# Routing counts of a capacity MoE with the operands swapped: eight-column float32r choices stationary, and the low parts of g moved to VectorE

## The chip, the core and the metric

One core of a Trainium2 chip runs the whole program. The metric is device time in microseconds (us) of one execution, from the first to the last instruction and a little around it. The engines are TensorE (PE, with its weight loads as PEld), VectorE (DVE), ScalarE (ACT), GpSimd (POOL) and SyncE (SP, which issues most DMAs).

## What is computed

Three layers follow one another on 1792 tokens: an attention with normalised queries and keys, a hardswish MLP (768 to 2048 to 768 features), and a mixture of 8 experts in which each expert takes at most 224 tokens.

```python
logits = x @ w_gate                       # 1792 x 8
order = np.argsort(-logits.flatten())
for idx in order:                         # best (token, expert) pairs first
    tok, e = idx // E, idx % E
    if assigned[tok] >= 0 or counts[e] >= cap:
        continue
    assigned[tok] = e
    counts[e] += 1
for e in range(E):
    mask = assigned == e
    out[mask] = np.maximum(x[mask] @ w1[e], 0.0) @ w2[e]
```

## The kernel before

Float32 products are made of float32r parts: a matrix is split into a high part (ScalarE copies it into float32r) and a low part (the difference), and three products high-high, high-low and low-high are added up.

The work runs in stages. Attention and the first MLP product are interleaved first. Then comes the second MLP product, called the y stage here: 14 tiles of 128 tokens, each with 16 blocks of 128 features, three products for each, in two column halves of 512 and 256 (`y_mm`, L1118). That is 14 x 16 x 3 x 2 = 1344 matmuls. Twelve tiles are done with both halves in turn; of the last two tiles first the 512-column halves are done, then the 256-column ones. Last come the experts.

The operand g of the y stage is read back from DRAM by `load_g` in units of four feature blocks (128 x 512 numbers). ScalarE makes the high part g2h (L1059), and GpSimd the low part g2l (L1061). There are two buffers for g2h and g2l, so g2h of a unit waits until TensorE has finished with the unit two before it. One unit feeds 24 y matmuls.

The routing (`routing`, L816 to L1026) is a Python generator that runs inside the y stage: each `yield` says how many y matmuls come before the next piece of routing on TensorE (the tuple `Y`, L62). TensorE's order is the order of the program text. The other engines' orders from the y stage on are planned at build time from estimated durations: an instruction that is ready may be put ahead of one that is not. On the chip each engine keeps its planned order.

The routing computes the greedy assignment by rounds: there are E - 1 = 7 of them and each fills one expert. A round finds each token's best open expert (`best`, giving the one-hot matrix A of 128 partitions x 14 token columns x 8 experts), turns the chosen logits into sortable keys of two 16-bit halves (kh, kl), and finds for all experts at once the largest key threshold at which some expert is full. Each half is found in three digits of 40 possible values. One digit is one step, so a round has 6 steps and the kernel 42:

- VectorE compares every key with 40 thresholds: C, 128 x 14 x 40 (L923).
- TensorE counts: 14 matmuls with C stationary (40 columns) and A moving (8 columns), giving 40 x 8 counts (L928).
- VectorE compares the counts with the room left: G, 40 x 8 (L930).
- TensorE adds G up over its 40 partitions and spreads the sum to 128 partitions, a matmul with `ones` (L933).
- VectorE takes the largest of 8 sums (js, L935), adds it to the prefix (L936), and shifts the thresholds (L921).

Before a step's counts stand Y[1] = 11 y matmuls, before its L933 Y[2] = 3. After six steps come counts above and at the threshold (L938 to L950), the choice of the expert and the ties (L953 to L972), and the update of what is open (L974 to L984), behind Y[3] = 16, Y[4] = 17 and Y[5] = 27 y matmuls. All counted numbers are small whole numbers, held in bfloat16. After the rounds the slots of the tokens are worked out (L986 to L1026). Per round 6 x 14 + 16 + 17 + 27 = 144 y matmuls are given, in all 30 + 7 x 144 + 10 + 20 = 1068. The routing starts when the router's logits are complete, 176 y matmuls into the stage, and has to end before the gather of the first expert's tokens, which needs the y of all tokens.

Of the kernel before, what the change touches and what calls it, by code (L numbers as in the profile page):

```python
# [8 lines left out]
F32 = mybir.dt.float32  # L9
# [12 lines left out]
def kernel(  # L22
# [39 lines left out]
    Y = (30, 11, 3, 16, 17, 27, 10, 20)  # L62
# [753 lines left out]
    def routing():  # L816
# [3 lines left out]
        DIG = ((40, (41 * 41, 41, 1)),) * 2  # L820
# [9 lines left out]
        tri = t_([128, 128], "tri", BF16)  # L830
        V.tensor_scalar(tri, jp[:, :128], 0.0, None, op0=OP.is_gt)
        ones = t_([128, 128], "ones", BF16)
        V.memset(ones, 1.0)
# [37 lines left out]
        V.tensor_copy(Lw, L)  # L871
        U = t_([128, NTC], "U")
# [12 lines left out]
        def best():  # L885
            m = t_([128, NTC], "m")
            V.tensor_reduce(m, Lw, axis=AX.X, op=OP.max)
            w = t_([128, NTC, E], "w")
            V.tensor_tensor(w, Lw, bc(m), op=OP.is_equal)
            V.tensor_tensor(w, w, be(e8), op=OP.mult)  # L890
            V.tensor_reduce(m, w, axis=AX.X, op=OP.max)
            A = t_([128, NTC, E], "A", BF16)
            V.tensor_tensor(A, w, bc(m), op=OP.is_equal)
            return A

        yield Y[0]
        for r in range(E - 1):
            A = best()
            w = t_([128, NTC, E], "w")
            kh = t_([128, NTC], "kh")  # L900
            kl = t_([128, NTC], "kl")
            V.tensor_tensor(w, A, hi, op=OP.mult)
            V.tensor_reduce(kh, w, axis=AX.X, op=OP.add)
            V.tensor_tensor(w, A, lo, op=OP.mult)
            V.tensor_reduce(kl, w, axis=AX.X, op=OP.add)
            V.tensor_tensor(kh, kh, U, op=OP.mult)
            found = []
            for key, (J, steps) in zip((kh, kl), DIG):
                if key is kl:
# [5 lines left out]
                p = t_([128, 1], "pre" + ("h" if key is kh else "l"))  # L915
                V.memset(p, 0.0)
                for i, x in enumerate(steps):
                    thr = jt[x][:, :J]
# [17 lines left out]
                    V.scalar_tensor_tensor(p, js, float(x), p, op0=OP.mult, op1=OP.add)  # L936
                found.append(p)
            gt = t_([128, NTC], "gt")  # L938
            ge = t_([128, NTC], "ge")
            V.tensor_scalar(gt, kl, found[1], None, op0=OP.is_gt)  # L940
            V.tensor_scalar(ge, kl, found[1], None, op0=OP.is_ge)
            rg = t_([128, 2, E], "rg")
# [3 lines left out]
            rgb = t_([128, 2, E], "rgb", BF16)  # L946
            V.tensor_copy(rgb, rg)
            yield Y[3]
            n = psum(128, 2 * E)
            nc.tensor.matmul(n, ones, rgb.rearrange("p a e -> p (a e)"), start=True, stop=True)  # L950
            es = t_([128, E], "es")
            m1 = t_([128, 1], "m1")
            V.tensor_tensor(es, n[:, E:], cap, op=OP.is_ge)  # L953
            V.tensor_tensor(es, es, e8, op=OP.mult)
            V.tensor_reduce(m1, es, axis=AX.X, op=OP.max)
            V.tensor_scalar(es, es, m1, None, op0=OP.is_equal)
            V.tensor_tensor(cap, cap, n[:, :E], op=OP.subtract)
# [4 lines left out]
            V.tensor_tensor(w, A, be(es), op=OP.mult)  # L962
            T = t_([128, NTC], "T")
            V.tensor_reduce(T, w, axis=AX.X, op=OP.add)
            V.tensor_tensor(ge, ge, gt, op=OP.subtract)
            V.tensor_tensor(T, T, ge, op=OP.mult)
            Tb = t_([128, NTC], "Tb", BF16)
            V.tensor_copy(Tb, T)
# [3 lines left out]
            nc.tensor.matmul(n, tri, Tb, start=True, stop=True)  # L972
            cc = t_([128, NTC, NTC], "cc")
# [4 lines left out]
            V.tensor_tensor(T, T, cum, op=OP.mult)  # L978
            V.tensor_tensor(gt, gt, T, op=OP.add)
            V.tensor_tensor(U, U, gt, op=OP.subtract)  # L980
            V.tensor_tensor(w, A, bc(gt), op=OP.mult)
            V.tensor_tensor(asg, asg, w, op=OP.add)
            V.scalar_tensor_tensor(cap, es, 9999.0, cap, op0=OP.mult, op1=OP.add)
            V.scalar_tensor_tensor(Lw, be(es), -3.0e38, Lw, op0=OP.mult, op1=OP.add)  # L984
            yield Y[5]
        A = best()  # L986
# [13 lines left out]
        tot = t_([128, E], "tot", BF16)  # L1000
# [25 lines left out]
        V.scalar_tensor_tensor(sidx, n[:, :2 * E], 128.0, lo, op0=OP.mult, op1=OP.add)  # L1026

# [88 lines left out]
    def y_mm(f, n, a, w, hf):  # L1116
# [8 lines left out]
        elif cnt[0] >= cnt[1]:  # L1125
            cnt[1] = cnt[0] + next(route, 10 ** 9)

# [186 lines left out]
```

## Time and profile before

| | |
|---|---|
| median of 3 runs | 1180.79 us (1177.22 to 1183.72) |
| the profiled execution, whole | 1180.09 us |
| its span, first to last instruction | 1178.2 us |
| mean granted TensorE clock | 0.985 of full speed |
| y stage, all of it | from 602.5 to 899 us |
| of it with routing, first count to slot numbers | from 646.8 to 883.3 us |

Times in the rows are microseconds from the first instruction. A group row gives busy time, mean duration of one instruction in ns, and the engine's idle time just before with what ended it. In a timeline a row with "x2" merges two instructions of the same kind. Matmuls are pipelined: the distance between starts is what one costs, not its duration.

### The profile page before, as it was taken

The page shows a single profiled execution, that of the slowest core. Times are in us where ns is not written, and L with a number is a line of the kernel's source. Part 1 is how long each engine was busy: PE and PEld are TensorE (multiplying, and loading weights), DVE is VectorE, ACT ScalarE, POOL GpSimd, SP SyncE. Part 2 cuts the span into 40 slices and gives each one's busy share as a digit, 9 for nine tenths or more (in the row PEclk, how much of TensorE's full clock was granted, in tenths as well). Part 3 has the DMA queues.
Part 4 walks back from the last instruction along what each step waited for, and adds up shares of the span by engine and source line. Part 5 has one row for each costly group of instructions (what it writes and reads, how often), then busy time and mean ns, then how long its engine had stood idle before and what let it go on. Part 6 is the DMA issues. An engine that isn't in the chain of part 4 may idle for free.

```text
span 1178.2 us, 19479 instructions
## 1 busy us (share of the span) xinstructions
PE 1114.9 (95%) x7204; PEld 903.5 (77%) x7204; DVE 707.3 (60%) x1485; ACT 519.4 (44%) x941; POOL 488.6 (41%) x363
## 2 busy tenths in 40 slices
PE   3988999999999999999999999999997999999997
PEld 2777765766766667787777777777777899999997
DVE  7887877886677844212432666666674756555560
ACT  3655655744545555543441111111123666565551
POOL 2211455663445533113452222222234577766540
PEclk9998999989999999999999999999999999999999
DMA  4365899978787887669995222222235888777731
GB/s 122 106 187 149 223 289 273 315 233 288 244 256 249 262 281 249 211 196 339 311 325 159 60 67 73 68 68 73 60 102 153 250 264 262 229 228 221 232 124 43
DMA packets 212678, 230.95 MB, mean 196 GB/s; under 512 B 26276, under 2 KB 185704, under 8 KB 212584
## 3 DMA queue, kind: packets, MB, share of 16 engines
q1 hardware_dynamic: 209256, 218.71, 60.3%
q0 software_dynamic: 3328, 11.01, 3.1%
q8 instruction: 56, 0.92, 0.3%
q14 instruction: 38, 0.31, 0.1%
HBM read 178.63 MB, written 51.04 MB: 195 GB/s over the span
## 4 chain that ended last, share of the span: by engine, by line
PE 71%; DVE 12%; DMA 7%; issue 5%; ACT 3%; POOL 2%; SPq 1%; POOLq 0%; DVEq 0%; ACTq 0%
PE y L1118 17%; PE h L528 17%; PE y L1266 8%; PE h L1202 5%; PE st L335 4%; PE av L424 3%; PE h L1204 3%; PE av L375 2%; PE rt L928 2%; DMA we_s<-in_moe_w_dram 2%; DMA w_hl<-w 2%; PE s L313 1%; DVE C L923 1%; PE lg L570 1%; DMA w<-cv 1%
## 5 line engine op out<-in xcount | busy, mean ns | idle before, releaser
L528 PE MATMUL h<-xh,w 128*128 128x448 f32 x768 | 241.7, 385 | 0.9 <-DVE mx L316 0.5
L528 PEld LDWEIGHTS h<-xh,w 128*128 128x128 f32 x768 | 144.3, 192 | 36.2 <-issue 21.9
L1061 POOL TENSOR_TENSOR g2l<-gr,g2h 128x512 fp32r<-128x512 f32 x60 | 78.8, 1315 | 190.2 <-ACT g2h L1059 154.9
L528 PE MATMUL h<-xl,w 128*128 128x448 f32 x384 | 146.8, 382 | 0.0
L1059 ACT ACTIVATE g2h<-gr 128x512 fp32r<-128x512 f32 x60 | 37.8, 631 | 221.6 <-PE y L1118 168.3
L316 DVE TENSOR_REDUCE mx<-s 112x1 f32<-112x448 f32 x192 | 105.7, 611 | 44.7 <-PE s L313 44.7
L1118 PE MATMUL y<-woh,g2l 128*128 128x512 f32 (+1 forms) x448 | 127.6, 347 | 1.0 <-POOL g2l L1061 1.0
L1118 PE MATMUL y<-woh,g2h 128*128 128x512 f32 (+1 forms) x448 | 126.8, 347 | 0.0
L1118 PE MATMUL y<-wol,g2h 128*128 128x512 f32 (+1 forms) x448 | 125.7, 345 | 0.0
L118 POOL TENSOR_TENSOR wel<-we_s,weh 128x768 fp32r<-128x768 f32 x48 | 97.8, 2041 | 42.7 <-ACT weh L117 31.9
L118 DVE TENSOR_TENSOR wel<-we_s,weh 128x768 fp32r<-128x768 f32 x59 | 79.3, 1350 | 58.3 <-ACT weh L117 58.1
L117 ACT ACTIVATE weh<-we_s 128x768 fp32r<-128x768 f32 x107 | 88.3, 840 | 56.7 <-DMA we_s<-in_moe_w_dram 40.4
L346 ACT ACTIVATE ph<-st 112x448 f32<-112x448 f32 x192 | 92.9, 544 | 44.6 <-PE st L335 43.8
L417 POOL TENSOR_TENSOR pa<-ph 112x448 f32<-112x448 f32 x68 | 85.7, 1282 | 41.6 <-ACT ph L346 41.6
L1202 PE MATMUL h<-xe,weh 128*128 128x448 f32 x318 | 100.4, 375 | 2.7 <-DVE xe L1153 2.7
L528 PEld LDWEIGHTS h<-xl,w 128*128 128x128 f32 x384 | 73.8, 192 | 12.4 <-issue 7.2
L1118 PEld LDWEIGHTS y<-woh,g2h 128*128 128x128 f32 x448 | 71.8, 188 | 11.8 <-issue 2.5
L1118 PEld LDWEIGHTS y<-woh,g2l 128*128 128x128 f32 x448 | 72.1, 188 | 11.1 <-POOL g2l L1061 1.3
L1118 PEld LDWEIGHTS y<-wol,g2h 128*128 128x128 f32 x448 | 71.7, 188 | 9.8 <-issue 0.7
L1204 PE MATMUL h<-xe,wel 128*128 128x224 f32 x318 | 76.6, 268 | 0.0
L531 ACT ACTIVATE r<-h,half 128x448 f32<-128x448 f32 x64 | 40.6, 635 | 80.5 <-PE h L528 70.2
L1266 PE MATMUL y<-weh,hl 128*112 128x384 f32 x216 | 72.9, 338 | 0.0
(244 smaller groups left out, 2311.4 us busy)
## 6 DMA issues: line engine op xcount, KB each, us to landing
we_s<-in_moe_w_dram SPq DMA_DIRECT2D x128, 384.0 KB, 3.9
w<-w_hl SPq DMA_DIRECT2D x32, 768.0 KB, 5.0
gr<-g_dr SPq DMA_DIRECT2D x52, 256.0 KB, 2.9
wraw<-in_moe_w_in_dram SPq DMA_DIRECT2D x16, 768.0 KB, 6.7
win_v<-w SPq DMA_DIRECT2D x32, 384.0 KB, 7.9
w_hl<-w SPq DMA_DIRECT2D x16, 768.0 KB, 5.5
wraw<-in_moe_w_out_dram SPq DMA_DIRECT2D x16, 768.0 KB, 5.5
g_dr<-g SPq DMA_DIRECT2D x48, 224.0 KB, 4.4
```

Source lines behind the costliest of these rows:

```text
L117: nc.scalar.activation(hi, raw, AF.Copy)
L118: eng.tensor_tensor(lo, raw, hi.bitcast(F32), op=OP.subtract)
L316: mx = nc.vector.tensor_reduce(MX[i][:, s, c:c + 1], pp[s][:CP, :S], axis=AX.X, op=OP.max)
L335: nc.tensor.matmul(pp[s][:CP, :S], a[r], b[r], start=(n == 0), stop=(n == len(todo) - 1))
L346: nc.scalar.activation(e, pp[s][:CP, :S], AF.Exp)
L417: nc.gpsimd.tensor_tensor(PA[i, s, n], PP[i, s, 2 * n][0], PP[i, s, 2 * n + 1][0], op=OP.add)
L528: nc.tensor.matmul(p[:, :S], lhs[:, c], x[:, c], start=(n == 0), stop=(n == 3 * NC - 1))
L1061: eng.tensor_tensor(gl, g, gh.bitcast(F32), op=OP.subtract)
L1118: nc.tensor.matmul(pp[hf][:, :COLS[hf].stop - COLS[hf].start], a[:, f % QF], w[:, COLS[hf]], start=(f == 0 and n == 0), stop=(f == NF - 1 ...
L1202: mm = [lambda: nc.tensor.matmul(p[:, :4 * CP], wh[:, fo], x.rearrange("d k t -> d (k t)"), start=(c == 0), stop=(c == NC - 1), skip_group ...
L1204: lambda: nc.tensor.matmul(p[:, :2 * CP], wl[:, fo], x[:, 0], start=False, stop=False, skip_group_check=True)]
L1266: nc.tensor.matmul(p[:CP, :HW], a[:, f, tk], w[:, o], start=(f == 0 and n == 0), stop=(f == FB - 1 and n == 2))
```

## The change

The roles in the counting matmul are exchanged: A is now stationary (128 x 8) and C moving (128 x 40), all in float32r. Before the 14 matmuls stands one that subtracts the room left (`capn` with `c128`), so that the counts are compared with zero. The comparison GZ is a 128 x 40 tile of which 8 partitions are written and the rest stay zero, and the matmul with `ones` uses all 128 partitions. VectorE then compares the sums with zero (g), adds up 40 numbers instead of taking the largest of 8, and subtracts the prefix inside the comparison that makes C, without shifting thresholds. In each round the update of the logits and the next `best` are issued behind the tie matmuls, before the ties are cut, and the two reductions of counts above and at the threshold become one over a tile of 2 x 14 x 8. While the routing runs the low parts of g are VectorE instructions, issued one at a time behind C, or forced when more than two wait; outside the routing GpSimd makes them as before. The y matmuls given become Y = (30, 12, 3, 12, 6, 31, 44, 22), with 4 more before the first count of the low half; in all 30 + 7 x (6 x 15 + 4 + 12 + 6) + 6 x 31 + 44 + 22 = 1066.

```diff
-    Y = (30, 11, 3, 16, 17, 27, 10, 20)
+    Y = (30, 12, 3, 12, 6, 31, 44, 22)
...
-                        thr = t_([128, JM], "thr")[:, :J]
-                        V.tensor_scalar(thr, jt[x][:, :J], p, None, op0=OP.add)
-                    C = t_([128, NTC, JM], "C", BF16)[:, :, :J]
-                    V.tensor_tensor(C, key[:, :, None].to_broadcast([128, NTC, J]),
-                                    thr[:, None, :].to_broadcast([128, NTC, J]), op=OP.is_ge)
-                    yield Y[1]
-                    n = psum(J, E)
+                        V.scalar_tensor_tensor(C, kb, p, jb, op0=OP.subtract, op1=OP.is_ge)
+                    else:
+                        V.tensor_tensor(C, kb, jb, op=OP.is_ge)
+                    if d == 0 and i == 0:
+                        kl = keys(A, lo, "kl")
+                    elif d == 0 and i == 1 and r:
+                        assign(*old)
+                    else:
+                        low_part()
+                    yield Y[1] + (4 if d and not i else 0)
+                    n = psum(E, JM)
+                    nc.tensor.matmul(n, capn[:, 1], c128[:, :JM], start=True, stop=False)
                     for c in range(NTC):
-                        nc.tensor.matmul(n, C[:, c, :], A[:, c, :], start=(c == 0), stop=(c == NTC - 1))
-                    G = t_([JM, E], "G", BF16)[:J]
-                    V.tensor_tensor(G, n, cap[:J], op=OP.is_ge)
+                        nc.tensor.matmul(n, AR[:, c, :], C[:, c, :], start=False, stop=(c == NTC - 1))
+                    V.tensor_scalar(GZ[:E], n, 0.0, None, op0=OP.is_ge)
                     yield Y[2]
-                    n = psum(128, E)
-                    nc.tensor.matmul(n, ones[:J, :], G, start=True, stop=True)
+                    n = psum(128, JM)
+                    nc.tensor.matmul(n, ones, GZ, start=True, stop=True)
+                    g = t_([128, JM], "g")
+                    V.tensor_scalar(g, n, 0.0, None, op0=OP.is_gt)
                     js = t_([128, 1], "js")
-                    V.tensor_reduce(js, n, axis=AX.X, op=OP.max)
+                    V.tensor_reduce(js, g, axis=AX.X, op=OP.add)
...
-            for i, x in enumerate((gt, ge)):
-                V.tensor_tensor(w, A, bc(x), op=OP.mult)
-                V.tensor_reduce(rg[:, i], w.rearrange("p c e -> p e c"), axis=AX.X, op=OP.add)
+            V.tensor_tensor(w2, A[:, None].to_broadcast([128, 2, NTC, E]),
+                            gg[:, :, :, None].to_broadcast([128, 2, NTC, E]), op=OP.mult)
...
+                V.tensor_reduce(rgb, w2.rearrange("p a c e -> p a e c"), axis=AX.X, op=OP.add)
...
+            nc.tensor.matmul(rn, c128, capn.rearrange("p a e -> p (a e)"), start=True, stop=False)
+            nc.tensor.matmul(rn, ones, rgb.rearrange("p a e -> p (a e)"), start=False, stop=True)
...
+            V.scalar_tensor_tensor(Tb, m, m1, ge, op0=OP.is_equal, op1=OP.mult)
...
             nc.tensor.matmul(n2, ones, Tb, start=True, stop=True)
             nc.tensor.matmul(n, tri, Tb, start=True, stop=True)
+            V.scalar_tensor_tensor(Lw, be(es), -3.0e38, Lw, op0=OP.mult, op1=OP.add)
+            old = A, gt
+            m, AR, A = best()
...
+    def low_part(eng=None, keep=1):
+        while len(lows) > keep:
+            gl, g, gh = lows.pop(0)
+            (eng or nc.vector).tensor_tensor(gl, g, gh.bitcast(F32), op=OP.subtract)
+            if eng is None:
+                break
...
-        eng = nc.gpsimd
-        eng.tensor_tensor(gl, g, gh.bitcast(F32), op=OP.subtract)
         GU[t, i] = gh, gl
+        lows.append((gl, g, gh))
+        if not routed[0]:
+            low_part(nc.gpsimd, 0)
+        elif len(lows) > 2:
+            low_part(nc.vector, 2)
```

## Rows read from the trace of the kernel before

**Rows 1.** The page, part 4: shares of the span in the chain that ended last.
```profile
PE y L1118 17%; PE h L528 17%; PE y L1266 8%; PE h L1202 5%; PE st L335 4%; PE av L424 3%; PE h L1204 3%; PE av L375 2%; PE rt L928 2%; DMA we_s<-in_moe_w_dram 2%; DMA w_hl<-w 2%; PE s L313 1%; DVE C L923 1%; PE lg L570 1%; DMA w<-cv 1%
```

**Rows 2.** By stretch: length, busy time of PE, PEld, DVE, ACT, POOL; clock, DMA share.
```profile
646.00:884.00 238.00, 231.81 (x1705) 184.39 (x1704) 155.07 (x533) 35.20 (x58) 62.11 (x48) 1.00 0.26 71
```

**Rows 3.** PE timeline of one step, 649.9 to 653.6: start, us, then the instruction.
```profile
649.86 0.40 PE L1118 MATMUL y<-wol,g2h 128*128 128x512 f32 x1
650.18 0.51 PE L928 MATMUL rt<-A,C 128*40 128x8 bf16 x14
650.62 0.39 PE L1118 MATMUL y<-wol,g2h 128*128 128x256 f32 x1
650.85 0.51 PE L1118 MATMUL y<-woh,g2l 128*128 128x512 f32 x2
651.29 0.18 PE L933 MATMUL rt<-G,ones 40*128 40x8 bf16 x1
651.39 0.62 PE L1118 MATMUL y<-woh,g2h 128*128 128x512 f32 x2
...
653.59 0.51 PE L928 MATMUL rt<-A,C 128*40 128x8 bf16 x14
```

**Rows 4.** The chain in order of time: y matmuls that nothing interrupts.
```profile
607.88 10.88 PE y L1118 x63
```

**Rows 5.** PEld timeline: weight loads of the counts, of y, of `ones`.
```profile
650.18 0.42 PEld L928 LDWEIGHTS <-C 128*40 128x40 bf16 x14 [0.25 <-issue]
650.62 0.19 PEld L1118 LDWEIGHTS y<-wol,g2h 128*128 128x128 f32 x1
668.45 0.10 PEld L950 LDWEIGHTS <-ones 128*128 128x128 bf16 x1 [0.17 <-issue]
```

**Rows 6.** Timeline: three full 128 x 128 transposes between y matmuls.
```profile
607.15 0.40 PE L1118 MATMUL y<-wol,g2h 128*128 128x512 f32 x1
607.17 0.47 PEld L596 LDWEIGHTS t<-ident,lgs 128*128 128x128 f32 x3
607.63 0.36 PE L1118 MATMUL y<-wol,g2h 128*128 128x256 f32 x1
607.84 0.40 PE L1118 MATMUL y<-woh,g2l 128*128 128x512 f32 x1
```

**Rows 7.** PE timeline, expert stage, float32r of 224 columns; chain: float32 of 66.
```profile
1026.04 0.26 PE L1204 MATMUL h<-xe,w 128*128 128x224 f32 x1
1026.14 0.37 PE L1202 MATMUL h<-xe,w 128*128 128x448 f32 x1
54.35 1.53 PE av L375 x16
```

**Rows 8.** PE's waits for other engines from 646 to 884: total, times, longest.
```profile
PE rt L928 <- DVE C L923: 3.0, 7, 0.4
PE rt L971 <- DVE Tb L968: 1.6, 1, 1.6
PE rt L1004 <- DVE tot L1001: 0.9, 1, 0.9
```

**Rows 9.** Timeline of DVE and POOL: C in a step undisturbed, and beside g2l.
```profile
648.78 0.74 DVE L923 TENSOR_TENSOR C<-kh,thr 128x560 bf16<-128x560 f32 x1
650.73 0.16 DVE L930 TENSOR_TENSOR G<-rt,cap 40x8 bf16<-40x8 f32 x1 [1.21 <-PE rt L928]
658.96 1.29 POOL L1061 TENSOR_TENSOR g2l<-gr,g2h 128x512 fp32r<-128x512 f32 x1 [4.51 <-ACT g2h L1059]
658.99 1.86 DVE L923 TENSOR_TENSOR C<-kl,thr 128x560 bf16<-128x560 f32 x1
```

**Rows 10.** A line's DVE instructions, the whole run: duration min/median/max in ns.
```profile
L118 DVE TENSOR_TENSOR wel<-we_s,weh x59: 942/959/3910, 890.8 to 1137.8; 128x768 fp32r<-128x768 f32 x59
```

**Rows 11.** DVE timeline from the tie matmuls to the next round's C.
```profile
672.12 0.36 DVE L974 TENSOR_TENSOR cc<-ctri,rt 128x196 f32<-128x196 f32 x1 [0.26 <-PE rt L972]
677.45 0.73 DVE L923 TENSOR_TENSOR C<-kh,jt 128x560 bf16<-128x560 f32 x1
```

More of the change, by code (lines that the diff above doesn't have):

```diff
@@ L828, in psum @@
             return ps.tile([128, 512], F32, name="rt", tag="b", bufs=8)[:p, :n]
-        tri = t_([128, 128], "tri", BF16)
+        tri = t_([128, 128], "tri", F32R)
         V.tensor_scalar(tri, jp[:, :128], 0.0, None, op0=OP.is_gt)
-        ones = t_([128, 128], "ones", BF16)
-        V.memset(ones, 1.0)
+        ones = t_([128, 128], "ones", F32R)
+        V.memset(ones.bitcast(F32), 1.0)
+        GZ = t_([128, JM], "GZ", F32R)
+        V.memset(GZ.bitcast(F32), 0.0)
+        c128 = t_([128, 128], "c128", F32R)
+        V.memset(c128.bitcast(F32), 1.0 / 128)
         ji = t_([128, JM], "ji", I32)
@@ L891, in best, with keys, assign @@
             V.tensor_reduce(m, w, axis=AX.X, op=OP.max)
-            A = t_([128, NTC, E], "A", BF16)
+            A = t_([128, NTC, E], "A", F32R, 2)
             V.tensor_tensor(A, w, bc(m), op=OP.is_equal)
-            return A
+            return m, A, A.bitcast(F32)
+        def keys(A, part, name):
+            w = t_([128, NTC, E], "w")
+            key = t_([128, NTC], name)
+            V.tensor_tensor(w, A, part, op=OP.mult)
+            V.tensor_reduce(key, w, axis=AX.X, op=OP.add)
+            return key
+        def assign(A, x):
+            w = t_([128, NTC, E], "w")
+            V.tensor_tensor(w, A, bc(x), op=OP.mult)
+            V.tensor_tensor(asg, asg, w, op=OP.add)
+        V.tensor_scalar(capn[:, 1], cap, -1.0, None, op0=OP.mult)
+        m, AR, A = best()
+        kh = keys(A, hi, "kh")
         yield Y[0]
         for r in range(E - 1):
[L898 to L905, printed above, removed]
             V.tensor_tensor(kh, kh, U, op=OP.mult)
             found = []
-            for key, (J, steps) in zip((kh, kl), DIG):
-                if key is kl:
+            for d, steps in enumerate(DIG):
+                if d:
                     hs = found[0]
@@ L914, in routing @@
                     V.tensor_tensor(kl, kl, t, op=OP.add)
-                p = t_([128, 1], "pre" + ("h" if key is kh else "l"))
-                V.memset(p, 0.0)
+                key = kl if d else kh
+                p = t_([128, 1], f"pre{d}")
                 for i, x in enumerate(steps):
-                    thr = jt[x][:, :J]
+                    C = t_([128, NTC, JM], "C", F32R)
+                    kb = key[:, :, None].to_broadcast([128, NTC, JM])
+                    jb = jt[x][:, None, :].to_broadcast([128, NTC, JM])
@@ L934, in routing @@
+                    g = t_([128, JM], "g")
+                    V.tensor_scalar(g, n, 0.0, None, op0=OP.is_gt)
                     js = t_([128, 1], "js")
-                    V.tensor_reduce(js, n, axis=AX.X, op=OP.max)
-                    V.scalar_tensor_tensor(p, js, float(x), p, op0=OP.mult, op1=OP.add)
+                    V.tensor_reduce(js, g, axis=AX.X, op=OP.add)
+                    if i:
+                        V.scalar_tensor_tensor(p, js, float(x), p, op0=OP.mult, op1=OP.add)
+                    else:
+                        V.tensor_scalar(p, js, float(x), None, op0=OP.mult)
@@ L946, in routing @@
-            rgb = t_([128, 2, E], "rgb", BF16)
-            V.tensor_copy(rgb, rg)
+            w2 = t_([128, 2, NTC, E], "wg2")
+            V.tensor_tensor(w2, A[:, None].to_broadcast([128, 2, NTC, E]),
+                            gg[:, :, :, None].to_broadcast([128, 2, NTC, E]), op=OP.mult)
+            rgb = t_([128, 2, E], "rgb", F32R)
+            with nc.allow_low_precision(reason="counts up to 14"):
+                V.tensor_reduce(rgb, w2.rearrange("p a c e -> p a e c"), axis=AX.X, op=OP.add)
@@ L948, in routing @@
+            V.tensor_tensor(ge, ge, gt, op=OP.subtract)
             yield Y[3]
-            n = psum(128, 2 * E)
-            nc.tensor.matmul(n, ones, rgb.rearrange("p a e -> p (a e)"), start=True, stop=True)
+            rn = psum(128, 2 * E)
+            nc.tensor.matmul(rn, c128, capn.rearrange("p a e -> p (a e)"), start=True, stop=False)
+            nc.tensor.matmul(rn, ones, rgb.rearrange("p a e -> p (a e)"), start=False, stop=True)
             es = t_([128, E], "es")
             m1 = t_([128, 1], "m1")
-            V.tensor_tensor(es, n[:, E:], cap, op=OP.is_ge)
@@ L977, in routing @@
             V.scalar_tensor_tensor(cum, n, rem, cum, op0=OP.subtract, op1=OP.is_lt)
-            V.tensor_tensor(T, T, cum, op=OP.mult)
+            T = t_([128, NTC], "T")
+            V.tensor_tensor(T, Tb.bitcast(F32), cum, op=OP.mult)
             V.tensor_tensor(gt, gt, T, op=OP.add)
             V.tensor_tensor(U, U, gt, op=OP.subtract)
[L981 to L986, printed above, removed]
+            if r < E - 2:
+                yield Y[5]
+        assign(*old)
         w = t_([128, NTC, E], "w")
@@ L999, in routing @@
             s = s2
-        tot = t_([128, E], "tot", BF16)
+        tot = t_([128, E], "tot", F32R)
         V.tensor_copy(tot, s[:, NTC - 1])
@@ L1125, in y_mm @@
         elif cnt[0] >= cnt[1]:
+            routed[0] = 1
             cnt[1] = cnt[0] + next(route, 10 ** 9)
+            if cnt[1] > 10 ** 8:
+                routed[0] = 0
+                low_part(nc.gpsimd, 0)
     XR, XE, got, EP = {}, {}, [None], []
```

27 lines of the change are left out of this document (14 added, 13 removed).

## Prediction

> **What bounds the kernel now.** I read the page's chain first: what ended last runs for 17% of the span through the y matmuls and for 2% through the counting matmuls [rows 1]. So a change inside the y stage counts in full where it shortens TensorE's own sequence, and hardly anywhere else. Then I read the stretch with the routing: 238 us, TensorE busy 231.8, VectorE 155.1, GpSimd 62.1, the clock at 1.00 of full speed [rows 2]. The reader should see that VectorE has some 80 us to spare and TensorE has 6. What TensorE waits for there, by the list of waits, is short: 3.0 us for C, 1.6 for Tb, 0.9 for tot [rows 8]. The waits are not the main cost. That is seen only in the timeline of one step: from one group of counts to the next, 650.18 to 653.59, pass 3.41 us for 14 y matmuls [rows 3]. Uninterrupted ones take 10.88 / 63 = 0.173 us each [rows 4], so 14 take 2.42. The other 0.99 us, 42 times, some 42 us in all, is what two small groups of matmuls cost TensorE.
>
> **Where the 0.99 us lie.** A pair of y matmuls (512 and 256 columns) takes 0.346 by [rows 4]; by its columns two thirds of it, 0.23, are the first's and 0.115 the second's. In [rows 3] the counts start 0.32 after a 512-column matmul, 0.09 late; 14 of them run until the next y at 650.62, 0.44; the next 256-column one takes 0.23, 0.11 too long. Sum 0.64. Around L933 the pair in front takes 0.44 (0.09 late) and the matmul with ones 0.10; the rest of the 0.99, 0.16, lies behind it, where the next y loads its weights anew as it does behind the counts. I round to 0.66 for the counts and 0.33 for the ones. The delay in front goes with the weight load: the loads of L928 and L950 begin only after 0.25 and 0.17 us of an idle loader [rows 5], so they did not run under the y matmul before them. The loads of the three full-width transposes did: the first begins at 607.17, while the y matmul of 607.15 streams, and the three cost 607.84 - 607.15 - 0.346 = 0.34, or 0.115 each, with hardly any delay in front [rows 6].
>
> **Part 1, the ones matmul.** It becomes 128 x 128 and float32r. I take it to behave like a transpose of [rows 6]: 0.115, and 0.13 with a small margin, instead of 0.33. That is 42 x 0.20 = 8.4 us less. Its bounds: 42 x 0.215 = 9.0 less, or, if the load still starts late and lasts as long as the y matmul's own load of that width and type (0.19 against 0.10 [rows 5], so 0.1 more), 42 x 0.1 = 4.2 more. The Trainium skill (TensorE: Matmul & The Clock Gate, section Weight-path perf modes) speaks against this part: the fast weight load needs 128 weights and a type that is not FP32, so the float32r ones would lose it. By that rule alone the sum would have the 4.2 more. No row here shows whether the load that is lost is also the one that can't overlap.
>
> **Part 2, the counts.** Fifteen pairs of load and matmul instead of 14. In the old group 14 loads take 0.42; less 0.10, about one load's own length, they follow each other by 0.32 / 13 = 0.025 us [rows 5]. An 8-column load is shorter than a 40-column one, and 40 float32r columns at the pace of 224 in 0.10 us [rows 7] are 0.018, both under 0.025. So I take 0.025: one pair more, 42 x 0.025 = 1.1 us. I leave the delays before and behind (0.09, 0.11), since the tile is as narrow as before. The bounds: float32, not float32r, of 66 columns on a 112-column load costs 1.53 / 16 = 0.096 a pair [rows 7], so 15 x 0.096 - 0.35 = 1.09 a step, 46 us more, at the far end; and if a narrow float32r load does overlap, 42 x 0.30 = 12.6 us less. I take the low value because the float32r row has over three times the 66 columns in the same time. The Trainium skill (FP8 and Floating Point Precision, TensorE Precision Notes) gives true FP32 four passes; with four passes 40 columns would be 0.067 by that page, an estimate. The float32r row of 224 columns shows one pass, and no row is narrower.
>
> **Part 3, rn and the ties.** Two more full-width matmuls take the place of one per round, and two others change type: by 0.115 each [rows 6] nothing or 0.1 less per round. I count 0.4 less.
>
> **Part 4, GpSimd's subtraction leaves.** In the fifth step of each round C takes 1.86 us instead of 0.74 while g2l runs on GpSimd [rows 9]. That is the wait of 3.0 us in seven times. With Tb and tot, 1.6 and 0.9, the waits are worth 5.5 [rows 8], and I take them all as gone: the cause leaves GpSimd, and tot gets 44 y matmuls of cover instead of 27 + 10.
>
> **Part 5, the subtraction comes to VectorE.** A subtraction of 768 columns takes 0.94 to 0.96 [rows 10], so one of 512 about 0.65; 48 of them are 31 us, into the 80 that are free. In a step VectorE pauses longest before G, 1.21 us [rows 9]. C ends at 649.52 [rows 9] and the counts start at 650.18 [rows 3]: 0.66 to spare. The new chain gains a comparison of 128 x 40 (g) and loses one (the thresholds), and 12 y matmuls stand instead of 11, so about 0.7 stay to spare. A low part that starts in the chain takes just this. One that starts just before G delays it: G ends at 650.89 [rows 9], L933 follows at 651.29 [rows 3], so 0.4 is hidden at most. Queued behind it on VectorE are GZ, g and C, and TensorE waits for these. Behind the last step cover falls from 16 y matmuls (2.8 us) to 12 (2.1), and for the choice of the expert from 17 to 6 (1.0). No wait is listed there in six of the seven rounds [rows 8], so the old chains fit into the old cover; the new ones are shorter by a product and a reduction, and by the second half of what stood before Tb, and I count 0.1 us a round as uncovered. Before the next round's first counts 43 y matmuls (7.4 us) cover a chain that took 6.1 before, from 672.12 to 678.18 [rows 11], and up to two low parts: full to the brim. I put 4 us for all this, 0.08 per low part; its ends are nothing and 31 us.
>
> **Nothing else moves.** All 1344 y matmuls stay, and the routing ends 2 y matmuls earlier than before, so gather and experts start right behind the same matmul. The builder plans VectorE, ScalarE and GpSimd anew, so their later order can move the end by a few us either way; that is in the range alone.
>
> **The sum.** -8.4 + 1.1 - 0.4 - 5.5 + 4.0 = -9.2 us. The profiled execution took 1180.09, which gives 1170.9. The median of the runs, 1180.79, lies 0.7 above that execution, within the scatter of the runs; I predict 1171.
>
> **The rivals.**
> - *The narrow load overlaps too.* Then the delays around the counts go as well: 12.6 less, 1158. For it stands that all types are now equal; against it that the matmul with 40 rows, L933, is as late as the one with 40 columns [rows 3], so a small tile seems enough. 10%.
> - *The ones load does not overlap.* Part 1 turns from -8.4 to +4.2: 1184, no change that can be told. For it stands that the bfloat16 ones of full width start late too (L950 [rows 5]); against it the transposes [rows 6]. This is also the case in which the change doesn't do what it says. 12%. The rule on fast weight loads in the Trainium skill, named above, would give this time.
> - *Low parts stand in the chain.* The order is planned ahead, and a low part that is ready goes into any pause. At 0.28 us of TensorE time per low part the gain is gone; at 0.4 it is 48 x 0.4 = 19 instead of 4: 1186. For it: an inserted 0.65 is as long as all that is spare. Against: two thirds of a step's time have room behind it. 18%, from 1176 to 1192.
> - *Slower: narrow float32r matmuls are slow.* The place is the counting group, the price 42 x 15 = 630 times what a pair takes above 0.025. At 0.040 a pair the gain of 9.2 is used up, and beyond it the change loses; at 0.060, between both rows, it costs 22 us: 1193. For it only float32 of 66 columns speaks [rows 7]; no float32r row is narrower than 224. 10%.
>
> **How the numbers follow.** The forecast has 45%, with its own range of 1164 to 1177; 5% stay for what I don't see. A measurement tells about 0.5% from no change, so the limits are 1174.9 and 1186.7. Faster: 0.40 of the forecast, the first rival, 0.05 of others, 0.55. Slower: the last rival and 0.10 of low parts and others, 0.20. Same: 0.25. The range of 1160 to 1188 leaves out the first rival and the last.
>
> **What the profile after would show.** Right: a step of 15 y matmuls lasts about 3.4 us, the loads of ones begin under the y matmul before, the counting group takes some 0.44, C stays at 0.74 in every step, and GpSimd has no g2l between 650 and 870. Wrong: counting matmuls further apart than 0.03, TensorE waits for GZ or C of over 0.1 us in many steps with a low part right ahead of them, or a late load of ones.

## The result and the profile after

| | before | after |
|---|---|---|
| median (6 runs each, same chip) | 1178.12 us | 1167.43 us |
| lowest and highest | 1177.21 to 1183.72 | 1164.15 to 1170.24 |
| profiled execution: span | 1178.2 us | 1168.3 us |

The ratio after to before is 0.9902, with a 95% interval of 0.9876 to 0.9929: some 10.7 us less. The forecast was 1171 with 1160 to 1188 around it. The total came out as forecast, but it is made of other parts, and much of what follows is about that.

The first view is the list of one line's instructions, here of y, first in the kernel before and then in the kernel after: its columns are count, shortest/median/longest duration in ns, and the start of the first and of the last one.

```profile
L1118 PE MATMUL y<-woh,g2h x448: 274/388/500, 602.5 to 896.9; 128*128 128x512 f32 x75, 128*128 128x256 f32 x75
L1155 PE MATMUL y<-woh,g2h x448: 274/386/499, 603.7 to 883.3; 128*128 128x512 f32 x75, 128*128 128x256 f32 x75
```

The y stage took 896.9 - 602.5 = 294.4 us before and takes 883.3 - 603.7 = 279.6 after. It became 14.8 us shorter, which is all of the difference and more. It began 1.2 us later, behind a part of the program that the change doesn't touch (across the profiles below the first y starts anywhere from 598.3 to 607.7), and behind the last y 3.8 us were lost again: from 897.2 to 1178.2 pass 281.0 us, from 883.5 to 1168.3 pass 284.8.

The second view is the timeline of one step after, rows of PE and PEld together, with some y rows left out; it answers to [rows 3, 5].

```profile
651.08 0.40 PE L1155 MATMUL y<-woh,g2l 128*128 128x512 f32 x1
651.08 0.09 PEld L946 LDWEIGHTS rt<-c,capn 128*8 128x8 f32 x1
651.31 0.18 PE L946 MATMUL rt<-c,capn 128*8 128x40 f32 x1
651.31 0.43 PEld L948 LDWEIGHTS rt<-C,A 128*8 128x8 f32 x14
651.70 0.37 PE L1155 MATMUL y<-woh,g2l 128*128 128x256 f32 x1
651.90 0.52 PE L1155 MATMUL y<-woh,g2h 128*128 128x512 f32 x2
652.14 0.19 PEld L952 LDWEIGHTS rt<-GZ,ones 128*128 128x128 f32 x1
652.26 0.18 PE L952 MATMUL rt<-GZ,ones 128*128 128x40 f32 x1
652.29 0.59 PE L1155 MATMUL y<-wol,g2h 128*128 128x512 f32 x2
...
654.46 0.18 PE L946 MATMUL rt<-c,capn 128*8 128x40 f32 x1
```

From 651.31 to 654.46 pass 3.15 us for 15 y, where 14 took 3.41. At 0.173 each, 15 y take 2.60, so the two small groups cost 0.55 instead of 0.98. Because 15 is odd, the counts fall behind a 512-column and a 256-column matmul by turns: such steps cost 0.56 and 0.67 us above their y, 0.61 in the mean. The load of ones (652.14) runs under y, as forecast. But so does the first load of the counts: 651.08, at the start of the y matmul, with no idle loader ahead of it, and the counts start 0.23 behind y instead of 0.32. They are 15 in 0.39 us, 0.026 each, and the next 256-column y takes 0.20, not 0.23.

The third view is what TensorE waited for from 640 to 885 (total us, times, longest), against [rows 8].

```profile
PE rt L991 <- DVE Tb L982: 2.0, 4, 1.3
PE y L1155 <- POOL g2l L1058: 1.2, 1, 1.2
PE rt L1029 <- DVE tot L1026: 1.0, 1, 1.0
PE rt L948 <- DVE C L935: 0.2, 1, 0.2
```

The wait for C, 3.0 us before, is nearly gone; those for Tb and tot are not (the one for g2l at the end of the stage was there before, with 1.0). The next rows give for a stretch its length, the busy time of PE, PEld, DVE, ACT and POOL, the clock, the DMA share and GB/s, against [rows 2]:

```profile
646.00:872.00 226.00, 222.46 (x1777) 190.62 (x1776) 149.75 (x541) 35.08 (x58) 2.58 (x2) 1.00 0.28 76
883.50:898.50 15.00, 10.74 (x54) 9.56 (x53) 7.01 (x10) 5.43 (x8) 5.27 (x7) 0.84 0.59 154
898.50:928.50 30.00, 26.25 (x149) 24.57 (x149) 21.73 (x28) 18.07 (x35) 16.51 (x11) 0.85 0.79 230
```

The first line is the routing: GpSimd's 62 us have left it, and VectorE is busy for 5 us less, though 46 subtractions, 32 us, came to it. The other two lines are the 45 us behind the last y. The same stretches of the kernel before:

```profile
897.20:912.20 15.00, 9.48 (x54) 8.45 (x52) 6.81 (x10) 4.90 (x8) 5.75 (x7) 0.91 0.58 145
912.20:942.20 30.00, 27.34 (x174) 25.68 (x173) 23.18 (x30) 19.98 (x38) 18.28 (x12) 0.99 0.88 251
```

The granted clock after was 0.85 in the second of them where it had been 0.99, and 149 instead of 174 matmuls were done in it. These are means of two levels, 2.4 and 1.2 GHz (1.00 and 0.50 in the column of the clock). In these 45 us TensorE ran at 1.2 GHz for 3.4 us in one stretch before, and for 13.6 us in three after. The first row is of the kernel before, the others of the kernel after:

```profile
909.60:913.01 3.41, 3.21 (x12) 3.03 (x13) 0.62 (x1) 0.54 (x1) 1.87 (x2) 0.50 0.61 173
886.95:890.36 3.41, 3.41 (x14) 3.15 (x14) 1.71 (x3) 0.84 (x1) 0.00 (x0) 0.50 0.99 235
897.19:900.60 3.41, 3.41 (x15) 3.15 (x13) 0.62 (x1) 0.36 (x1) 1.82 (x2) 0.50 0.65 172
910.85:917.67 6.82, 5.39 (x18) 5.00 (x19) 6.82 (x11) 4.41 (x9) 5.88 (x6) 0.50 0.90 254
```

In the chain an expert's matmul of 448 columns takes 0.40 us there and 0.21 at the full clock. In the kernel after the first fall comes behind the pause in which TensorE waits for the first expert's tokens (xe). That pause, before and after:

```profile
899.00 0.47 PE L1202 MATMUL h<-xe,w 128*128 128x448 f32 x1 [1.53 <-DVE xe L1153]
885.84 0.47 PE L1243 MATMUL h<-xe,w 128*128 128x448 f32 x1 [2.05 <-DVE xe L1194]
```

Before, the clock stayed at its full level behind the pause of 1.53 and fell at 909.60, behind a later one. Counted from the last y, the 100th matmul came 0.5 us later after than before, and the 160th 3.8 us later, which is the whole loss. TensorE's pauses of over 0.5 us in these 45 us add up to nearly the same, 8.2 us before and 8.0 after. What remains is the clock: TensorE was busy at 1.2 GHz for 3.2 us before and 12.2 after. At half speed half of the 9.0 us more are lost, an estimate of 4.5 us against the 3.8 measured.

This loss is not scatter. In the profiles of the kernel before and its three variants below, TensorE runs at 1.2 GHz for 3.4 to 6.8 of these 45 us, and 280.4 to 281.0 us pass from the last y to the end. In the changed kernel and its seven variants it is 10.2 to 13.7 us, and 283.1 to 284.8 to the end. The first pause for xe is at most 1.53 us in the first four and 1.94 to 2.56 in the other eight. So the changed kernel costs 2 to 4 us behind its own stage.

### The profile page after: what moved, and what is told of

It reads as the page before. It is cut to its first block, busy times and chain, and to the rows that moved or that the text cites. A ratio compares the mean times of both kernels' runs of the same rounds, so it can differ in the third digit from the quotient of the medians.

```text
span 1168.3 us, 19514 instructions
## 1 busy us (share of the span) xinstructions
PE 1104.3 (95%) x7253; PEld 908.8 (78%) x7253; DVE 716.6 (61%) x1493; ACT 518.7 (44%) x941; POOL 426.3 (36%) x317
## 4 chain that ended last, share of the span: by engine, by line
PE 69%; DVE 10%; DMA 9%; issue 5%; ACT 4%; POOL 2%; SPq 1%; POOLq 0%; DVEq 0%; ACTq 0%
PE y L1155 19%; PE h L528 15%; PE y L1307 8%; PE h L1243 6%; PE st L335 4%; PE h L1245 3%; PE av L424 3%; PE av L375 2%; DMA w_hl<-w 2%; DMA sum_dr<-rb 2%; DVE cv L142 1%; PE rt L948 1%; PE lg L570 1%; DVE mx L316 1%; ACT ph L346 1%
## 5 line engine op out<-in xcount | busy, mean ns | idle before, releaser
L1093 ACT ACTIVATE g2h<-gr 128x512 fp32r<-128x512 f32 x60 | 37.7, 631 | 205.9 <-PE y L1155 160.5
L1155 PE MATMUL y<-woh,g2l 128*128 128x512 f32 (+1 forms) x448 | 125.1, 345 | 1.2 <-POOL g2l L1058 1.2
L118 DVE TENSOR_TENSOR wel<-we_s,weh 128x768 fp32r<-128x768 f32 x59 | 89.3, 1520 | 55.6 <-ACT weh L117 43.7
L1058 POOL TENSOR_TENSOR g2l<-gr,g2h 128x512 fp32r<-128x512 f32 x14 | 18.2, 1304 | 232.3 <-ACT g2h L1093 232.2
L1155 PEld LDWEIGHTS y<-woh,g2l 128*128 128x128 f32 x448 | 72.0, 189 | 10.7 <-POOL g2l L1058 1.4
```

Of the source, the lines that this page charges most:

```text
L118: eng.tensor_tensor(lo, raw, hi.bitcast(F32), op=OP.subtract)
L1155: nc.tensor.matmul(pp[hf][:, :COLS[hf].stop - COLS[hf].start], a[:, f % QF], w[:, COLS[hf]], start=(f == 0 and n == 0), stop=(f == NF - 1 ...
```

## The experiments

Beside the median and the ratio to the kernel before on the same chip, two readings of each profile are used, because whole times scatter by some 5 us around a change of a few. One is the **y stage** (first to last start of `y<-woh,g2h`; 294.4 before, 279.6 after). The other is the **overhead** of an undisturbed step, one in which TensorE waits for nothing: the distance between the first counting matmuls of two steps in the PE timeline less 0.1734 per y (0.98 before, 0.56 and 0.67 by turns after). Each kernel has one profile.

| kernel | median, us | ratio, 95% | y stage, us | overhead of a step, us |
|---|---|---|---|---|
| after | 1167.43 | 0.9902 [0.9876, 0.9929] | 279.6 | 0.56 / 0.67 |
| counts_bf16 | 1171.39 | 0.9946 [0.9926, 0.9967] | 285.1 | 0.73 / 0.85 |
| ones_bf16 | 1168.94 | 0.9908 [0.9887, 0.9930] | 278.8 | 0.55 / 0.67 |
| ones_8rows | 1175.29 | 0.9971 [0.9956, 0.9986] | 289.5 | 0.87 / 0.97 |
| before_counts_f32r | 1179.52 | 0.9997 [0.9984, 1.0009] | 294.3 | 0.95 |
| before_ones_pad | 1170.43 | 0.9918 [0.9892, 0.9945] | 284.8 | 0.80 |
| before_lows_dve | 1172.94 | 0.9959 [0.9939, 0.9979] | 288.9 | 0.98 |
| lows_pool | 1162.58 | 0.9878 [0.9824, 0.9932] | 278.1 | 0.56 / 0.66 |
| low_later | 1166.37 | 0.9898 [0.9852, 0.9943] | 279.4 | 0.56 / 0.66 |
| low_later_y | 1164.38 | 0.9871 [0.9830, 0.9913] | 276.9 | 0.56 / 0.66 |
| lows_pool_y | 1164.62 | 0.9878 [0.9856, 0.9899] | 276.3 | 0.56 / 0.67 |

**Why the counts' load runs ahead: their type, or their 8 columns.** Two kernels ask this, one from either side. In the changed kernel:

```diff
-            A = t_([128, NTC, E], "A", F32R, 2)
+            A = t_([128, NTC, E], "A", BF16, 2)
...
-                    C = t_([128, NTC, JM], "C", F32R)
+                    C = t_([128, NTC, JM], "C", BF16)
...
-                    nc.tensor.matmul(n, capn[:, 1], c128[:, :JM], start=True, stop=False)
+                    nc.tensor.matmul(n, capb, cb, start=True, stop=False)
```

> The changed kernel with its counting operands in bfloat16; the stationary choices keep their 8 columns. In the changed kernel the loads of the counting group begin under the y matmul before, and a step of 15 y matmuls takes 3.15 us; in the kernel before they begin late. Type theory (a weight load runs ahead only where its type is that of the y matmuls, float32r): the load of the first choice begins late again, a step takes 3.15 + about 0.2 = 3.35 to 3.4 us, 42 times, so 8 to 10 us more: 1176 to 1178. Shape theory (8 columns are loaded ahead, 40 are not): steps stay at 3.15, time 1167 to 1168.

From the timeline of counts_bf16, PE and PEld, the start of a group of counts:

```profile
680.61 0.39 PE L1160 MATMUL y<-woh,g2h 128*128 128x512 f32 x1
680.93 0.08 PEld L950 LDWEIGHTS <-capb 128*8 128x8 bf16 x1 [0.25 <-issue]
680.93 0.18 PE L950 MATMUL rt<-cb,capb 128*8 128x40 bf16 x1
681.40 0.38 PE L1160 MATMUL y<-woh,g2h 128*128 128x256 f32 x1
```

The loader is idle for 0.25 us again, the counts start 0.32 behind y, and the group takes 0.47 instead of 0.39. The overhead rises by 0.17 us a step, the stage by 5.5 us, the ratio by 0.44%, some 5 us. The mechanism is that of the type theory, with half of the price that was expected in the total. The other side is the kernel before, where the 40 stationary columns stay:

```diff
-            A = t_([128, NTC, E], "A", BF16)
+            A = t_([128, NTC, E], "A", F32R)
...
-                    C = t_([128, NTC, JM], "C", BF16)[:, :, :J]
+                    C = t_([128, NTC, JM], "C", F32R)[:, :, :J]
```

> The kernel before with its counting operands in float32r: the stationary comparisons keep their 40 columns, all else stays, the bfloat16 ones too. Type theory: the delays before and behind the counting group (0.09 + 0.11, with their like at the next group) go, a step of 14 y matmuls falls from 3.41 to 3.1 or 3.2 us, 42 times: 9 to 12 us less, about 1168. Shape theory: a step stays at 3.41 and the time at 1178. If float32r matmuls of 8 moving columns were slow in themselves, the 14 would stand further apart than 0.026 us.

```profile
661.84 0.39 PE L1118 MATMUL y<-woh,g2h 128*128 128x512 f32 x1
661.89 0.75 PEld L928 LDWEIGHTS rt<-A,C 128*40 128x40 f32 x14
662.07 0.67 PE L928 MATMUL rt<-A,C 128*40 128x8 f32 x14
662.59 0.36 PE L1118 MATMUL y<-woh,g2h 128*128 128x256 f32 x1
```

The result has something in it that neither theory had. The load does begin under y (661.89) and the counts start 0.23 behind it, as the type theory has it; yet time and stage don't move. From 662.07 to 662.59 the 14 pairs take 0.52 us, 0.037 each, against 0.44 in bfloat16 [rows 3]. What the early start gives, the slower pairs take back. So alone the type is worth 0.03 of overhead and the exchange of the roles 0.01 (bfloat16 with 8 stationary columns has 0.79 in the mean, bfloat16 with 40 and the cheap ones of before_ones_pad 0.80). Both together are worth 0.19 a step: early start and 0.026 a pair. The exchange makes the stationary side narrower and the moving side wider at once; which of the two brings 0.026 instead of 0.037 was not tried.

**What made the ones cheap: type, or padding to 128 rows.** Three kernels ask this. The first makes the ones and their answers bfloat16:

```diff
-        GZ = t_([128, JM], "GZ", F32R)
+        GZ = t_([128, JM], "GZ", BF16)
...
-                    nc.tensor.matmul(n, ones, GZ, start=True, stop=True)
+                    nc.tensor.matmul(n, onesb, GZ, start=True, stop=True)
```

> The changed kernel with bfloat16 ones and flags in the small sum; the ones stay 128 x 128 and the flags padded to 128 rows. Type theory: the load of ones begins only after the y matmul before it has ended, the group takes about 0.25 to 0.33 instead of 0.12 us, 42 times: 5 to 9 us more, 1173 to 1176. Shape theory (full width is loaded ahead whatever its type): no change, 1167 to 1168.

The second takes only the 8 rows that count, in float32r:

```diff
-                    nc.tensor.matmul(n, ones, GZ, start=True, stop=True)
+                    nc.tensor.matmul(n, ones[:E], GZ[:E], start=True, stop=True)
```

> The changed kernel without the padding: the small sum is made from the 8 rows of ones and of flags that count, float32r as before. If a load of few rows can't begin under a y matmul (rows theory), the group takes about 0.33 instead of 0.12 us, 42 times: 8 to 9 us more, 1176. If only the type decides, it stays at 0.12 and the time at 1167 to 1168: the padding was then for nothing.

The third pads the kernel before:

```diff
+        G = t_([128, E], "G", BF16)
+        V.memset(G, 0.0)
...
-                    G = t_([JM, E], "G", BF16)[:J]
-                    V.tensor_tensor(G, n, cap[:J], op=OP.is_ge)
+                    V.tensor_tensor(G[:J], n, cap[:J], op=OP.is_ge)
...
-                    nc.tensor.matmul(n, ones[:J, :], G, start=True, stop=True)
+                    nc.tensor.matmul(n, ones, G, start=True, stop=True)
```

> The kernel before with the answers padded to 128 rows (88 rows of zeros) and the whole 128 x 128 tile of ones loaded; both stay bfloat16. Rows theory (a load of fewer than 128 rows can't begin under a matmul, nor can the next load begin under its own): the group of ones falls from 0.33 to about 0.13 us, 42 times: 8 us less, 1169 to 1170, and a step of 14 y matmuls lasts 3.2 us. If the rows matter only together with float32r: a step stays at 3.41 and the time at 1177 to 1178.

The group of ones in the timeline, first of ones_bf16, then of ones_8rows:

```profile
662.79 0.40 PE L1157 MATMUL y<-wol,g2h 128*128 128x512 f32 x1
663.02 0.10 PEld L954 LDWEIGHTS <-onesb 128*128 128x128 bf16 x1 [0.16 <-issue]
663.03 0.19 PE L954 MATMUL rt<-GZ,onesb 128*128 128x40 bf16 x1
663.07 0.36 PE L1157 MATMUL y<-wol,g2h 128*128 128x256 f32 x1
```

```profile
660.66 0.39 PE L1155 MATMUL y<-wol,g2h 128*128 128x512 f32 x1
660.98 0.18 PEld L952 LDWEIGHTS rt<-GZ,ones 8*128 8x128 f32 x1 [0.25 <-issue]
660.98 0.28 PE L952 MATMUL rt<-GZ,ones 8*128 8x40 f32 x1
661.19 0.19 PEld L1155 LDWEIGHTS y<-wol,g2h 128*128 128x128 f32 x1
661.19 0.39 PE L1155 MATMUL y<-wol,g2h 128*128 128x256 f32 x1
```

The load of the full tile in bfloat16 starts late, behind 0.16 us of an idle loader, and that costs nothing: its matmul stands 0.24 behind y and the next y 0.04 behind it. With 8 rows and the same float32r, the matmul stands 0.32 behind y, and the next y, whose load begins only with it at 661.19, 0.21 behind the small one: 0.31 more a step, and 9.9 us in the stage. So it is the rows and not the type. before_ones_pad shows it from the side of before: with nothing but 88 rows of zeros a step falls from 0.98 to 0.80 of overhead, in all 35 distances between steps within a round.

The third kernel shows one thing more. Its 35 steps lost 9.8 us of overhead (37.7 to 27.9), of which 35 x 0.18 = 6.3 are the ones. The other 3.5 come from the wait for the fifth step's C in each round, 0.5 us before ([rows 9] has this C) and now gone, although the subtractions are still on GpSimd. The two instructions still meet:

```profile
752.44 0.74 DVE L925 TENSOR_TENSOR C<-kl,thr 128x560 bf16<-128x560 f32 x1
752.49 1.83 POOL L1062 TENSOR_TENSOR g2l<-gr,g2h 128x512 fp32r<-128x512 f32 x1 [4.35 <-ACT g2h L1060]
```

Here C starts 0.05 us ahead and takes its 0.74, and GpSimd takes 1.83 instead of 1.29. In [rows 9] GpSimd started 0.03 ahead, and C took 1.86. The one that starts second stands behind the first. This is so in all seven rounds of either kernel, and the eight slow C of lows_pool below all end 0.60 us behind the end of a subtraction that had started before them. The Trainium skill (GPSIMD Engine Reference, section Specifications) says that GpSimd shares its SBUF interfaces with VectorE, with contention where VectorE has two SBUF inputs, as C has. The trace agrees, with 0.74 against 1.86, and adds that the order of the starts says who pays.

**What the move of the low parts is worth.** It is undone in the changed kernel, and made alone in the kernel before, where `routed` is set while the routing runs.

```diff
-        if not routed[0]:
+        if True:
             low_part(nc.gpsimd, 0)
```

> The changed kernel with every low part of g left on GpSimd. In the changed kernel the 28 steps of 15 y matmuls inside the rounds lose 3.3 us against the shortest of them, the round changes 1.9, and two waits of the last round 2.3. Contention theory (what the move bought is a VectorE undisturbed by GpSimd): C takes 1.86 us again beside a subtraction on GpSimd, the waits for C come back with about 3 us, and the time is 1169 to 1172. Chain theory (the low parts in VectorE's queue cost what the move saved or more): the 3.3 and 1.9 us go for the larger part and the time is 1163 to 1166. Both true: 1167 to 1168, the move was worth nothing.

```diff
-        eng = nc.gpsimd
+        eng = nc.vector if routed[0] else nc.gpsimd
```

> The kernel before with only the low parts of g moved to VectorE while the routing runs. If contention with GpSimd makes the fifth step of each round 0.5 us longer and the move cures that alone: 7 x 0.5 = 3.5 us less, 1174.5. If the low parts delay the chains as much: 1177 to 1179. If each stands in the chain for 0.4 us: 1190.

Alone the move is worth 5.5 us of stage and 0.4% of time: 3.5 in the fifth steps, 1.2 at the six changes of rounds (10.3 to 9.1 above their y), and 0.8 outside of both. In the changed kernel it is worth nothing or a little less than nothing: with GpSimd doing the subtractions the stage is 1.5 us shorter (after and low_later, whose VectorE does nearly the same work, differ by 0.2). The medians differ by 5, but the intervals of the two ratios overlap, so only the stage is used here. C is slow again there in 8 of the 42 steps (the longest in the row below, 1.8 us), and yet TensorE waits for C 1.0 us in all:

```profile
L935 DVE SCALAR_TENSOR_TENSOR C<-kl,pre,jt x14: 800/802/1765, 655.8 to 837.8; 128x560 fp32r<-128x560 f32 x14
```

The last kernel of this group puts the low parts later:

```diff
-    def low_part(eng=None, keep=1):
+    def low_part(eng=None, keep=2):
...
-        elif len(lows) > 2:
-            low_part(nc.vector, 2)
+        elif len(lows) > 3:
+            low_part(nc.vector, 3)
...
+            if k == 2 and routed[0] and len(lows) > 2:
+                low_part(nc.vector, 2)
```

> The changed kernel with each low part of g put into VectorE's order about a third of a unit of y later, behind the moment when its high part can be written, so that VectorE doesn't stand at it. In the changed kernel VectorE waits up to 2.2 us for a high part of g in two steps, which last 0.5 us longer than the shortest, and less in some more. If this waiting is what the excess of the steps consists of: 2 to 4 us less, 1163 to 1165. If the excess comes from the work itself (0.69 us in the chain wherever it stands): no change, 1166 to 1168.

What this was aimed at stands in the timeline of the kernel after:

```profile
708.11 0.63 ACT L1093 ACTIVATE g2h<-gr 128x512 fp32r<-128x512 f32 x1 [3.12 <-PE y L1155]
708.30 0.52 PE L948 MATMUL rt<-C,A 128*8 128x40 f32 x14
708.77 0.69 DVE L1058 TENSOR_TENSOR g2l<-gr,g2h 128x512 fp32r<-128x512 f32 x1 [2.20 <-ACT g2h L1093]
709.38 0.18 DVE L949 TENSOR_SCALAR GZ<-rt 8x40 fp32r<-8x40 f32 x1
709.62 0.29 PE L952 MATMUL rt<-GZ,ones 128*128 128x40 f32 x1
```

The counts are done at about 708.8, but VectorE has stood at a low part since 706.6, whose high part ScalarE can write only when y has left the buffer, and GZ comes 0.5 us late. The experiment didn't change that. In its profile the same wait of 2.20 stands in the same step: VectorE's order on the chip is the same as before the edit but for one low part less at the end of the routing and one neighbouring pair exchanged. The order is planned from estimated times, and that the plan undid the edit is the likely reason. The run says nothing for or against either expectation. What can be said is the size: the 35 steps inside the rounds cost 23.5 us of overhead in the kernel after, 21.4 if all were undisturbed, so such delays are 2.1 us. The four longest steps (0.85 to 1.09) all have a low part right ahead of GZ.

**The cover at the change of rounds.** Cover is the number of y matmuls that TensorE has to do while VectorE prepares the next piece of routing.

```diff
-    Y = (30, 12, 3, 12, 6, 31, 44, 22)
+    Y = (30, 12, 3, 12, 10, 27, 44, 22)
```

> The same as the run before it, with 10 y matmuls instead of 6 between the choice of the expert and the sums of Tb, and 27 instead of 31 at the end of a round. The waits for Tb (2.0 us in four rounds) should go, and the first counts of the next round still have 39 y matmuls of cover. If the cover decides: 1 to 2 us less than the run before it; if what is taken from the end of the round is missed there: a wait for C at each round's first counts, 1 to 3 us more.

> The changed kernel with all low parts on GpSimd and with 10 y matmuls instead of 6 between the choice of the expert and the sums of Tb (27 instead of 31 at the end of a round). With the low parts on GpSimd the y stage took 278.3 us, of which the first two round changes lose 2.5 against the later ones. If the cover of 6 y matmuls is what they lack: 2 to 3 us less in the y stage, 276, and a time of 1160 to 1162. If the end of the round then lacks cover for the next first C: the stage stays at 278 and the time at 1163.

Over 6 y, 1.0 us, Tb wasn't ready in four rounds; over 10 it is in all but one, and the wait for C stays at 0.3. The wait for Tb falls from 2.3 in low_later to 0.3, and 2.5 us leave the stage (279.4 to 276.9), a little more than expected. With GpSimd doing the low parts 1.8 us leave it (278.1 to 276.3), and the stage is the shortest of all. Both kernels lie below the one after by median (1164.4 and 1164.6), but in whole time neither is told apart from it, and the 1160 to 1162 expected of lows_pool_y were missed: three of its six runs lie at 1161.5 to 1162.4, the other three at 1166.8 to 1167.1.

## Why the forecast held, point by point

- **The bound, and the 0.98 us around two small groups:** right. All that the change gained, it gained there and in the waits of the y stage.
- **Part 1, ones, -8.4:** right in size, 42 x 0.18 = 7.6 by before_ones_pad (ones_8rows, with 8 rows in place of 40, gives 9.9). The mechanism was half right: what counts is that all 128 rows are loaded, and the type is free. So the second rival had no ground: it took the late start of the bfloat16 ones for a cost, and a late start at full width costs nothing (0.04 us to the next y). The Trainium skill (TensorE: Matmul & The Clock Gate, section Weight-path perf modes) has the load of such a tile faster outside FP32. The trace agrees, with float32r on the side of FP32 (0.10 against 0.19), but under a y matmul of 0.23 that doesn't matter.
- **Part 2, counts, +1.1:** wrong, and the largest miss. Measured (0.61 - 0.80) x 42 = -8.0. The step that failed is "I leave the delays before and behind (0.09, 0.11), since the tile is as narrow as before". The 0.025 a pair was right (0.026). In these runs the delays go with bfloat16 of fewer than 128 columns, or with fewer than 128 rows, and the new tile is neither. The first rival, held at 10%, was this case: 9.1 of the 12.6 us that it gave came, and its 1158 was missed because of what follows. Its argument against (L933 is as late) compared a tile of 40 rows with one of 40 columns, two things with two causes.
- **Part 4, waits, -5.5:** 2.3 came: C fell from 3.0 to 0.2, but Tb stayed (1.6 to 2.0) and tot too (0.9 to 1.0). That the waits were all taken as gone is the step that failed. Tb has 6 y of cover instead of 17, and the added low parts stand ahead of it; in the last round one of them waits for a high part whose g comes late from DRAM. Why tot waits over 44 y was not tried; without low parts ahead of it, in lows_pool, it waits 1.4. The wait for Tb in the last round:

```profile
849.11 1.15 ACT L1093 ACTIVATE g2h<-gr 128x512 fp32r<-128x512 f32 x2 [1.84 <-DMA gr<-g_dr]
849.77 0.69 DVE L1058 TENSOR_TENSOR g2l<-gr,g2h 128x512 fp32r<-128x512 f32 x1 [1.61 <-ACT g2h L1093]
851.06 0.28 PE L991 MATMUL rt<-Tb,ones 128*128 128x14 f32 x1 [1.27 <-DVE Tb L982]
```

  And the wait for C hung on which of two instructions started 0.03 us earlier: by before_ones_pad it would have gone with the ones alone.
- **Part 5, low parts, +4.0:** right in size: 2.1 in the steps and up to 1.8 at the changes of rounds, shared with Tb's cover (six cost 10.0 above their y; six like the undisturbed ones, 1.36, would cost 8.2; with 10 y of cover they cost 8.5, so most of the 1.8 is cover). That is under 0.09 for each of the 46 (not 48), so the rival in which they stand in the chain, from 0.28, was far.
- **"Nothing else moves":** right for the range, wrong for the sum: 1.2 ahead of the stage and 3.8 behind it. The 3.8 go with the clock behind the last y, at 0.84 and 0.85 where it was 0.91 and 0.99, which the prediction left to its range.
- **The last rival,** slow pairs: 0.026 against the 0.040 from which it would have decided.
- **The signs named beforehand:** the loads of ones begin under y, as said. A step lasts 3.15 us instead of 3.4 and the counting group 0.39 instead of 0.44, both because of part 2. C takes 0.74 or, in its new form, 0.80, and none is stretched. GpSimd has one g2l between 650 and 870, at 858.95.
- **The sum.** The 35 steps inside the rounds fell from 37.7 us of overhead to 23.5: ones -6.3, counts 35 x -0.19 = -6.6, the fifth steps -3.5, delays by low parts +2.1. The six changes of rounds, where the same two groups should have given 6 x 0.37 = 2.2, hardly moved (10.3 to 10.0): Tb and the low parts took it, by the two runs with 10 y of cover mostly Tb. That is 14.5 of the stage's 14.8. Against the forecast of -9.2 the counts brought 9.1 more, the waits 3.2 less, and 5.0 were lost outside the stage: -10.1, and the two profiled executions are 10.0 apart. With the terms of the stage alone, the forecast would have been 1180.1 - 14.8 = 1165.3. The number held because misses of both signs met, and that was luck.

## What to carry to other kernels

A small matmul between large ones cost here not its columns but two gaps. Whether there are gaps is seen in the loader's idle time ahead of its load together with the distance to the next large matmul. Filling the tile of ones up to 128 rows with zeros closed them at no cost, in float32r and in bfloat16; with 8 or 40 columns 128 rows were enough in float32r only. Change type and shape together before judging either: here each alone was worth 0.03 us a step or less, and both 0.19. Where two engines meet at the same time in every round, ask which one starts first and by how much: a loss that hangs on 0.03 us can go or come with any change of the loop. And look behind the stage that was changed: here it gave a quarter of its gain back to a lower clock.

## What was not expected of the hardware

- A load of fewer than 128 rows never ran under the y matmul before it in these steps (8 rows float32r and 40 rows bfloat16: loader idle for 0.25 us, next matmul 0.32 behind y), nor did one of 128 rows in bfloat16 with 8 or 40 columns (0.25 and 0.32 too). In float32r with 128 rows it ran ahead at 8, 40 and 128 columns (0.23 to 0.24 behind y). The Trainium skill (TensorE: Matmul & The Clock Gate, section LDWEIGHTS) says that a load's time goes with its columns and not its rows. The load of 8 x 128 lasts 0.18 and that of 128 x 128 0.19, so the trace agrees on the duration; but when it begins went here with its rows and its type. The cause of this was not found.
- Pairs of load and matmul stood 0.026 us apart in float32r with 8 stationary and 40 moving columns, and 0.037 with the roles exchanged.
- Of two instructions of VectorE and GpSimd that meet, the later one paid nearly the whole (C 1.86 or g2l 1.83, never both).
- Behind the y stage the granted clock was 0.84 to 0.85 for 45 us in the kernel after, where it had been 0.91 and then 0.99, with the same pauses in all. It goes with the kernel: 3.4 to 6.8 us at 1.2 GHz in the four profiles of the kernel before and its variants, 10.2 to 13.7 in the eight of the changed one. The eight also have the longer first pause for xe; that this pause is the cause is not shown (in counts_bf16 it is 2.17 us, and the first fall comes only 11.2 us behind the last y), because no run changed the work behind the stage.
